# A decode attention kernel: one exponential per group of heads, the head masks as products, and output scaling on GpSimd

## The chip, the cores and the metric

The kernel runs on one core of one Trainium2 chip. The metric is device time in microseconds for one execution. The core's engines work side by side and wait for each other through semaphores: TensorE (PE in the profile, with its weight loads as PEld), VectorE (DVE), ScalarE (ACT), GpSimd (POOL) and SyncE (SP), which here issues nearly all transfers. Sixteen DMA engines move the data.

## The reference, cut to what matters

One token (B = S = 1) of width 512 passes through an attention block A over a window of W = 4096 cached keys and values, with 32 heads of width 128 and no sharing of heads, and through a small MLP block B whose result gates A's.

```python
xn = layernorm(x)
q = (xn @ wq).reshape(32, 128)
k, v = k_cache[:, Sk - 4096:, :], v_cache[:, Sk - 4096:, :]     # 32 heads each
scores = einsum("hd,hkd->hk", q, k) * 128 ** -0.5
o = einsum("hk,hkd->hd", softmax(scores), v)
s = o.reshape(4096) @ wo
out = x + s * silu(B(xn, w1, w2, w3, w4))
```

The window of K and of V is 33.5 MB each in bf16, the weights are about 12 MB, and each byte is used once.

## The kernel before, in words

**Groups.** The 32 heads are worked in 8 groups of G = 4. One K tile (`kv` in `k_pool`, three buffers) holds the 4096 keys of four heads: partition p belongs to head p mod 4 of the group and holds CP = 128 consecutive keys of 128 numbers, 4 MB in all. V has the same layout, with two buffers. The mask `par` (128 x 4) is 1 where the partition is of that head.

**Scores.** In `k_vector` DVE does 64 or 80 of the 128 keys of each partition, in four parts: a product K x q (L321) and a reduction over the 128 numbers (L323), into columns of the tile S. The rest goes through PE: `k_turn` transposes keys (L339), ACT copies them out of PSUM (L342), and `k_scores` multiplies them with q (L350) into `sT`, in which each partition holds its keys' scores with all four heads of the group, of which only its own head's is wanted.

**Softmax.** `sm_own` (L359, four ACT products) multiplies `sT` with the mask `par`, and `sm_max` adds the four up into S (L364, DVE) and takes each partition's maximum (L366). `sm_turn` transposes the maxima (L372, PE), takes the maximum of each head (L374) and writes it, scaled, into the first row of `md` (L376). `sm_exp` multiplies `md` with `par_t` on PE (L381): each partition gets four biases, one for each head, and for the three heads that aren't its own the bias is about −1e30, so that their exponentials are zero. ACT copies the biases (L384) and does four exponentials with sums (L388) into `pT`. `sm_den` adds the sums over the partitions (L394, PE) and `sm_rden` takes the reciprocals (L399, DVE).

**Values.** `v_wide` (L427) multiplies pT with V on PE, ACT copies the result (L433), `v_turn` transposes it (L444), `v_add` adds up the diagonal pieces into `oT` (L450, DVE), and `v_out` scales with `rden`: groups 0 to 2 by four ACT products (L475), groups 3 to 7 by one DVE product (L471). The last 32 columns of the last group use narrow matmuls instead (`v_part`, L461).

**Output.** `ox_spread` (L482, DVE), `ox_pick` (L490 PE; L492, L496 DVE) and `y_wide` (L518, PE) multiply blocks of 16, 8 and 4 heads with wo. The last four heads go through `y_head`. A product with the gate and a sum with x end the kernel.

**Order.** The order on PE, DVE and ACT is written out by hand (`tc.manual_schedule`); GpSimd's and SP's is not in that list. The loop over s = 0 to 9 does the scores of group s and the values of group h = s − 2. One step is, for DVE: K part 0, `sm_rden(s-2)`, K part 1, the two small instructions of `sm_turn(s-1)`, K part 2, `v_add(h-1)`, `v_out(h-1)`, in step 6 `ox_spread(0)`, K part 3, in step 6 the DVE part of `ox_pick(0)`, `sm_max(s)`. Step 7 takes `v_add` and `v_out` of groups 4 and 5, and `ox_spread(1)` follows the latter, before `sm_max(7)`. Step 8 begins with the pick of block 1 and `sm_turn(7)`, `sm_exp(7)`. SP issues the loads in program order (`load`, L76); a load into a buffer waits until its old contents have been read. One PSUM buffer (`misc`) serves the maxima, biases, denominators and transposed outputs in turn.

**Memory.** `pad` is an unused tile that moves what is allocated behind it.

Of the kernel before, what the change touches and what calls it, by code (L numbers as in the profile page):

```python
# [8 lines left out]
P = 128  # L9
BF16 = mybir.dt.bfloat16  # L10
FP32 = mybir.dt.float32
ACT = mybir.ActivationFunctionType
ALU = mybir.AluOpType
AX = mybir.AxisListType
# [4 lines left out]
G = 4  # L19
# [7 lines left out]
def kernel(  # L27
# [14 lines left out]
    nc = tc.nc  # L42
# [25 lines left out]
    ps_o = ctx.enter_context(tc.tile_pool(name="ps_o", bufs=1, space=PSUM))  # L68
    ps_y = ctx.enter_context(tc.tile_pool(name="ps_y", bufs=1, space=PSUM))
    sm_pool = ctx.enter_context(tc.tile_pool(name="sm", bufs=3))  # L70
    small.tile([P, 96], BF16, name="pad")
    wts_guard = tc.tile_pool(name="wts", bufs=1)
    wts = wts_guard.__enter__()

# [44 lines left out]
    ind = const.tile([P, 1], FP32, name="ind")  # L119
    nc.vector.tensor_reduce(out=ind[:], in_=ident_f[:, 0:P:32], axis=AX.X, op=ALU.max)  # L120
    neg_half = const.tile([P, 33], FP32, name="neg_half")
    nc.vector.memset(neg_half[:], -0.5)

# [102 lines left out]
                           in_=qt_ps[rows].bitcast(BF16).rearrange("p g (a m l) -> p g a m l", a=G, l=2)[:, :, :, 0, :])  # L226

    shifted_bf = small.tile([P, KC], BF16, name="shifted_bf")
    nc.vector.memset(shifted_bf[:], 0.0)
    hs_ps = ps_misc.tile([P, KC], FP32, tag="misc", name="hs_ps")  # L230
    for j in range(KC):
        for c in range(KC):
# [35 lines left out]
    for i, (col, w) in enumerate(terms):  # L268
# [26 lines left out]
    par = const.tile([P, G], FP32, name="par")  # L295
    nc.vector.tensor_reduce(out=par[:], in_=ident_f[:].rearrange("p (b a) -> p a b", a=G), axis=AX.X,
                            op=ALU.max)
    par_t = const.tile([1 + G, PB, G], FP32, name="par_t")
    nc.vector.tensor_scalar(out=par_t[:],
                            in0=ident_f[0:1 + G, 1:1 + G].unsqueeze(1).to_broadcast([1 + G, PB, G]),  # L300
                            scalar1=ident_f[0:1 + G, 0:1], scalar2=None, op0=ALU.add)
    md = const.tile([1 + G, G], FP32, name="md")
    nc.vector.tensor_scalar(out=md[:], in0=ident_f[0:1 + G, 1:1 + G], scalar1=-1.0, scalar2=1e30,
                            op0=ALU.add, op1=ALU.mult)

    st = {}

    def nd(g):
        return 64 if g == 0 or g >= LATE else 80

    def k_open(g):
        st[g] = {
            "sT": ps_s.tile([P, CP - 64, G], FP32, tag="sT", name="sT"),
            "S": sm_pool.tile([P, CP], FP32, tag="S", name="S"),
        }

    def k_vector(g, kn, part):
# [33 lines left out]
                                 lhsT=kt[:, i, l::2], rhs=q_pair[:, g, l, :], start=(l == 0), stop=(l == 1))  # L351


    def sm_own(g):
        s = st[g]
        m = CP - nd(g)
        s["own"] = sm_pool.tile([P, CP - 64, G], FP32, tag="own", bufs=1, name="own")
        for a in range(G):
            nc.scalar.mul(s["own"][:, 0:m, a], s["sT"][:, 0:m, a], par[:, a:a + 1])  # L359

    def sm_max(g):
        s = st[g]
        n = nd(g)
        nc.vector.tensor_reduce(out=s["S"][:, n:CP], in_=s["own"][:, 0:CP - n, :], axis=AX.X, op=ALU.add)  # L364
        s["m1"] = sm_pool.tile([P, 1], FP32, tag="m1", name="m1")
        nc.vector.tensor_reduce(out=s["m1"][:], in_=s["S"][:], axis=AX.X, op=ALU.max)  # L366

    def sm_turn(g):

        s = st[g]  # L370
        mt_ps = ps_misc.tile([1, P], FP32, tag="misc", name="mt_ps")
        nc.tensor.transpose(mt_ps[:], s["m1"][:], ident_f[:])  # L372
        mx = sm_pool.tile([1, G], FP32, tag="mx", name="mx")
        nc.vector.tensor_reduce(out=mx[:], in_=mt_ps[:].rearrange("r (b a) -> r a b", a=G), axis=AX.X,  # L374
                                op=ALU.max)
        nc.vector.tensor_scalar(out=md[0:1, :], in0=mx[:], scalar1=-scale, scalar2=None, op0=ALU.mult)  # L376

    def sm_exp(g):
        s = st[g]
        mb_ps = ps_misc.tile([P, G], FP32, tag="misc", name="mb_ps")  # L380
        nc.tensor.matmul(mb_ps[:], lhsT=par_t[:].rearrange("k b a -> k (b a)"), rhs=md[:], start=True,  # L381
                         stop=True)
        mb = sm_pool.tile([P, G], FP32, tag="mb", name="mb")
        nc.scalar.copy(out=mb[:], in_=mb_ps[:])  # L384
        s["pT"] = sm_pool.tile([P, CP, G], BF16, tag="pT", name="pT")
        s["sum"] = sm_pool.tile([P, G], FP32, tag="sum", name="sum")
        for a in range(G):
            nc.scalar.activation(out=s["pT"][:, :, a], in_=s["S"][:], func=ACT.Exp, scale=scale,  # L388
                                 bias=mb[:, a:a + 1], accum_out=s["sum"][:, a:a + 1])

    def sm_den(g):
        s = st[g]
        s["den"] = ps_misc.tile([P, G], FP32, tag="misc", name="den_ps")
        nc.tensor.matmul(s["den"][:], lhsT=ones_f[:], rhs=s["sum"][:], start=True, stop=True)  # L394

    def sm_rden(g):
        s = st[g]
        s["rden"] = sm_pool.tile([P, G], FP32, tag="rden", name="rden")
        nc.vector.reciprocal(out=s["rden"][:], in_=s["den"][:])  # L399


# [44 lines left out]
    def v_add(g):  # L446
        s = st[g]
        if g < NG - 1:
            s["oT"] = sm_pool.tile([P, G], FP32, tag="oT", name="oT")
        nc.vector.tensor_reduce(out=s["oT"][:], in_=s["ot"][:].rearrange("p (x m) -> p m x", m=32)[:, 0:G, :],  # L450
                                axis=AX.X, op=ALU.add)

# [11 lines left out]
    def v_out(g):  # L464
        h = G * g
        b = [i for i, (h0, _) in enumerate(blocks) if h >= h0][-1]
        if b not in o_blk:
            o_blk[b] = sm_pool.tile([P, blocks[b][1]], BF16, tag=f"o{b}", bufs=1, name="o")
        c = h - blocks[b][0]
        if g >= NG - 5:  # L470
            nc.vector.tensor_tensor(out=o_blk[b][:, c:c + G], in0=st[g]["oT"][:], in1=st[g]["rden"][:],  # L471
                                    op=ALU.mult)
            return
        for k in range(G):
            nc.scalar.mul(o_blk[b][:, c + k:c + k + 1], st[g]["oT"][:, k:k + 1], st[g]["rden"][:, k:k + 1])  # L475


    def ox_spread(i):
# [52 lines left out]
    for s in range(NG + LAG):  # L531
# [22 lines left out]
        if s < NG:  # L554
            nb = len(batches(s))

            def keys(b0, b1):
                for b in range(b0, b1):
                    k_turn(s, kn, b)
                    if b > 0:  # L560
                        k_scores(s, b - 1)

            k_open(s)
            k_vector(s, kn, 0)
            keys(0, 2)
            if s == 7:
                v_turn(h - 1)
                v_add(h - 1)
                v_out(h - 1)
            elif s > 1:  # L570
                sm_den(s - 2)
                sm_rden(s - 2)
            elif s == 1:
                sm_max(0)
            k_vector(s, kn, 1)
            keys(2, 4)
            if s == 7:
                sm_den(h)
                sm_rden(h)
                keys(4, nb - 2)  # L580
                sm_turn(s - 1)
                keys(nb - 2, nb)
            else:
                if s > 0:
                    sm_turn(s - 1)
                keys(4, nb)
            k_scores(s, nb - 1)
            sm_own(s)
            if s == 7:
                k_vector(s, kn, 2)  # L590
                v_wide(h, v)
                sm_exp(s - 1)
                v_turn(h)
                y_open()
                k_vector(s, kn, 3)
                v_add(h)
                v_out(h)
                ox_spread(1)
                sm_max(s)
                continue  # L600
            if s > 0:
                sm_exp(s - 1)
            if h > 0:
                v_turn(h - 1)
            k_vector(s, kn, 2)
            if h >= 0:
                v_wide(h, v)
            if h > 0:
                v_add(h - 1)
                v_out(h - 1)  # L610
            if s == 6:
                ox_spread(0)
            k_vector(s, kn, 3)
            if s == 6:
                ox_pick(0)
            if s > 0:
                sm_max(s)
        elif s == NG:
            ox_pick(1)
            sm_turn(NG - 1)  # L620
            sm_exp(NG - 1)
            y_wide(1, False)
            sm_den(NG - 2)
            sm_rden(NG - 2)
            y_wide(0, False)
            warm(3)
            v_wide(h, v)
            sm_den(NG - 1)
            sm_rden(NG - 1)
            v_turn(h)  # L630
            v_add(h)
            v_out(h)
            ox_spread(2)
        else:
            v_open(h)
            warm(3)
            v_wide(h, v, cuts[1], last=False)
# [47 lines left out]
```

## Time and profile before

| | before |
|---|---|
| time, median of 3 runs | 193.25 us (193.23 to 193.55) |
| span of the profiled execution | 191.2 us |
| PE / PEld busy | 116.4 us (61%) / 74.2 us (39%) |
| DVE busy | 150.9 us (79%), 175 instructions |
| ACT busy | 89.2 us (47%), 191 instructions |
| POOL busy | 2.3 us (1%), 11 instructions |
| DMA | 79.02 MB, mean 413 GB/s |

The page gives the profiled execution by its span, from the first instruction to the end of the last; it states no device time of that same execution beside it. The median of the three timed runs is 2.05 us above the span. Rows of groups read: line, engine, operation, output <- inputs, shapes, count | busy us, mean ns of one | idle time before them and what ended it. Rows in order of time read: start us, duration us, then the same, with idle time before it in brackets. In windows, the busy time of each engine in that stretch stands with its count of instructions.

### The profile page before, as it was taken

What the parts mean: (1) busy time and instruction counts of PE and PEld (TensorE: products, weight loads), DVE (VectorE), ACT (ScalarE), POOL (GpSimd) and SP (SyncE); (2) the same over time, 40 slices, a digit from 0 to 9 for tenths busy, and PEclk for the clock granted to TensorE, in tenths of its full rate; (3) what the DMA queues carried; (4) which work ended last, traced back from release to release, by engine and by line L of the source; (5) the groups of instructions that cost most, each with busy time, mean ns of one, the idle gap of its engine ahead of it and who ended that gap; (6) DMA issues with size and microseconds to landing.
All of it is one profiled execution on the core that took longest, in us unless ns stands there. A gap on an engine that the chain in (4) does not pass through costs nothing.

```text
span 191.2 us, 2839 instructions
## 1 busy us (share of the span) xinstructions
PE 116.4 (61%) x1159; PEld 74.2 (39%) x1159; DVE 150.9 (79%) x175; ACT 89.2 (47%) x191; POOL 2.3 (1%) x11
## 2 busy tenths in 40 slices
PE   1653754989825368256845772680888189739762
PEld 0430222767614334143334441540763077313322
DVE  1660159979999999999999999999999999980111
ACT  2001370888794076427464564542475148733120
POOL 2110000000000000000000000000000000000000
PEclk9999695555755557955695588557567858975998
DMA  6999999999999999999999999999999998999990
GB/s 211 447 430 404 431 418 439 439 439 437 432 434 439 432 429 432 432 439 432 422 432 432 418 422 418 452 439 435 439 432 434 435 432 372 471 425 405 420 371 32
DMA packets 4572, 79.02 MB, mean 413 GB/s; under 512 B 624, under 2 KB 1232, under 8 KB 1488
## 3 DMA queue, kind: packets, MB, share of 16 engines
q1 hardware_dynamic: 4264, 74.65, 91.6%
q10 hardware_dynamic: 296, 4.20, 5.1%
q8 instruction: 9, 0.15, 0.3%
q14 instruction: 3, 0.02, 0.0%
HBM read 78.84 MB, written 0.00 MB: 412 GB/s over the span
## 4 chain that ended last, share of the span: by engine, by line
DVE 46%; DMA 43%; PE 5%; ACT 3%; issue 1%; SPq 1%; ACTq 0%; DVEq 0%
DMA kv<-in_A_k_cache_dram 31%; DVE S L323 28%; DVE prod L321 15%; DMA kv<-in_A_v_cache_dram 10%; ACT kt L342 3%; DMA x_bf<-in_A_x_dram 2%; PE pt L339 2%; PE ov L427 1%; DVE m L366 1%; DVE S L364 1%; SPq L76 1%; PE sT L350 1%; DVE mx L374 1%; PE oT L461 1%; PE ot_ps L444 0%
## 5 line engine op out<-in xcount | busy, mean ns | idle before, releaser
L323 DVE TENSOR_REDUCE S<-prod 128x20 f32<-128x2560 bf16 (+1 forms) x32 | 86.0, 2686 | 1.1
L342 ACT COPY kt<-pt 128x1024 bf16<-128x1024 bf16 x52 | 51.2, 1013 | 40.4 <-PE pt L339 38.7
L339 PE MATMUL pt<-ident_f,kv 128*128 128x128 f32 x208 | 46.7, 376 | 10.8 <-DMA kv<-in_A_k_cache_dram 10.8
L321 DVE TENSOR_TENSOR prod<-kv,q_bc 128x2560 bf16<-128x2560 bf16 (+1 forms) x32 | 45.4, 1418 | 3.9 <-DMA kv<-in_A_k_cache_dram 3.7
L339 PEld LDWEIGHTS pt<-ident_f,kv 128*128 128x128 f32 x208 | 34.2, 196 | 14.4 <-DMA kv<-in_A_k_cache_dram 10.5
L350 PE MATMUL sT<-q_pair,kt 128*128 128x8 bf16 x416 | 19.4, 170 | 15.7 <-ACT kt L342 15.5
L350 PEld LDWEIGHTS <-kt 128*128 128x128 bf16 x416 | 16.4, 104 | 26.8 <-ACT kt L342 25.8
L427 PE MATMUL ov<-kv,pT 128*16 128x512 bf16 x248 | 22.0, 515 | 1.4 <-DMA kv<-in_A_v_cache_dram 1.4
L388 ACT ACTIVATE pT<-S,mb 128x128 bf16<-128x128 f32 x32 | 13.9, 573 | 0.3
L372 PE MATMUL mt_ps<-ident_f,m 128*1 128x128 f32 x8 | 2.9, 359 | 17.4 <-DVE rden L399 16.9
L433 ACT COPY ov_sb<-ov 128x512 f32<-128x512 f32 x8 | 4.7, 586 | 17.1 <-PE ov L427 17.1
L427 PEld LDWEIGHTS <-pT 128*16 128x16 bf16 x248 | 6.9, 109 | 13.2 <-issue 11.4
L359 ACT ACTIVATE own<-sT,par 128x48 f32<-128x48 f32 (+1 forms) x32 | 7.5, 356 | 3.7 <-PE sT L350 3.7
L444 PE MATMUL ot_ps<-ident_f,ov_sb 128*128 128x128 f32 x32 | 7.1, 359 | 2.9 <-ACT mb L384 1.9
L211 DVE CAST q_row<-qr_ps 128x512 bf16<-128x512 f32 x1 | 0.7, 692 | 9.9 <-PE qr_ps L208 9.9
L388 ACT ACTIVATION_READ_ACCUMULATOR pT<-S,mb 128x1 f32 x32 | 8.3, 258 | 0.0
L372 PEld LDWEIGHTS mt_ps<-ident_f,m 128*1 128x1 f32 x8 | 0.6, 80 | 17.9 <-DVE rden L399 17.2
L399 DVE RECIPROCAL rden<-den_ps 128x4 f32<-128x4 f32 x8 | 1.4, 175 | 7.0 <-PE den_ps L394 7.0
L381 PE MATMUL mb_ps<-md,par_t 5*128 5x4 f32 x16 | 3.9, 311 | 4.1 <-DVE md L376 4.1
L255 ACT ACTIVATE a_row<-a_ps 128x384 bf16<-128x384 f32 x1 | 0.5, 491 | 12.0 <-remote 12.0
L444 PEld LDWEIGHTS ot_ps<-ident_f,ov_sb 128*128 128x128 f32 x32 | 4.5, 178 | 3.9 <-ACT mb L384 2.3
L208 PE MATMUL qr_ps<-wq_sb,xq_bf 128*1 128x512 bf16 x32 | 3.1, 566 | 3.7 <-DMA wq_sb<-in_A_wq_dram 3.7
(122 smaller groups left out, 81.6 us busy)
## 6 DMA issues: line engine op xcount, KB each, us to landing
kv<-in_A_k_cache_dram SPq DMA_DIRECT2D x7, 4096.0 KB, 31.3
kv<-in_A_v_cache_dram SPq DMA_DIRECT2D x7, 4096.0 KB, 30.6
wq_sb<-in_A_wq_dram ACTq DMA_DIRECT2D x1, 4096.0 KB, 17.6
kv<-in_A_k_cache_dram SPq DMA_DIRECT2D x2, 2048.0 KB, 27.4
wo<-in_A_wo_dram SPq DMA_DIRECT2D x1, 2048.0 KB
kv<-in_A_v_cache_dram SPq DMA_DIRECT2D x1, 2048.0 KB
kv<-in_A_v_cache_dram SPq DMA_DIRECT2D x2, 1024.0 KB, 17.6
w_sb<-in_B_w_dram SPq DMA_DIRECT2D x1, 1376.0 KB, 9.1
```

The lines of the kernel that those rows point to most:

```text
L321: nc.vector.tensor_tensor(out=prod[:, 0:m, :], in0=kn[:, rows, :], in1=q_bc[:, g:g + 1, :].to_broadcast([P, m, Dh]), op=ALU.mult)
L323: nc.vector.tensor_reduce(out=st[g]["S"][:, rows], in_=prod[:, 0:m, :], axis=AX.X, op=ALU.add)
L339: nc.tensor.transpose(pt[:, i, :], kn[:, c:c + 2, :].rearrange("p c d -> p (c d)").bitcast(FP32), ident_f[:])
L342: nc.scalar.copy(out=kts[b][:, 0:n, :], in_=pt[:, 0:n, :].bitcast(BF16))
L350: nc.tensor.matmul(st[g]["sT"][:, c:c + 2, :].rearrange("p c a -> p (c a)"), lhsT=kt[:, i, l::2], rhs=q_pair[:, g, l, :], start=(l == 0), ...
L359: nc.scalar.mul(s["own"][:, 0:m, a], s["sT"][:, 0:m, a], par[:, a:a + 1])
L372: nc.tensor.transpose(mt_ps[:], s["m1"][:], ident_f[:])
L381: nc.tensor.matmul(mb_ps[:], lhsT=par_t[:].rearrange("k b a -> k (b a)"), rhs=md[:], start=True, stop=True)
L388: nc.scalar.activation(out=s["pT"][:, :, a], in_=s["S"][:], func=ACT.Exp, scale=scale, bias=mb[:, a:a + 1], accum_out=s["sum"][:, a:a + 1])
L427: nc.tensor.matmul(ov[r:r + 4 * G], lhsT=s["pT"][:, c:c + 4, :].rearrange("p i a -> p (i a)"), rhs=v[:, c:c + 4, :], start=(i < 4), stop=( ...
L433: nc.scalar.copy(out=s["ov_sb"][:], in_=ov[:])
L444: nc.tensor.transpose(ot_ps[:, step * j:step * j + P], s["ov_sb"][:, j, :], ident_f[:])
```

## The change

- `sm_exp`: the bias is one number for each partition, its own head's maximum. One exponential with one sum gives `e`, and four ACT products of `e` with the columns of `par` give `pT`.
- `sm_turn` writes the scaled maxima 32 times over ([1, 32, 4]) so that one matmul brings each partition its own; `par_t` and `md` go.
- `sm_den`: each partition has one sum; the sums are broadcast as weights and multiplied with `par`.
- `sm_own` goes. `sm_max` multiplies `sT` with `par` in one DVE product before it adds up.
- `v_out`: groups 0 to 5 are scaled by one GpSimd product, groups 6 and 7 by DVE.
- `S`, `rden` and `oT` get eight buffers each; two memsets at the start go from DVE to GpSimd; `pad` is longer.

```diff
-    small.tile([P, 96], BF16, name="pad")
+    small.tile([P, 208], BF16, name="pad")
...
-    nc.vector.memset(neg_half[:], -0.5)
+    nc.gpsimd.memset(neg_half[:], -0.5)
...
-    nc.vector.memset(shifted_bf[:], 0.0)
+    nc.gpsimd.memset(shifted_bf[:], 0.0)
...
-    par_t = const.tile([1 + G, PB, G], FP32, name="par_t")
-    nc.vector.tensor_scalar(out=par_t[:], ...)
-    md = const.tile([1 + G, G], FP32, name="md")
-    nc.vector.tensor_scalar(out=md[:], ...)
...
-            "S": sm_pool.tile([P, CP], FP32, tag="S", name="S"),
+            "S": sm_pool.tile([P, CP], FP32, tag="S", bufs=NG, name="S"),
...
-    def sm_own(g):
-        s = st[g]
-        m = CP - nd(g)
-        s["own"] = sm_pool.tile([P, CP - 64, G], FP32, tag="own", bufs=1, name="own")
-        for a in range(G):
-            nc.scalar.mul(s["own"][:, 0:m, a], s["sT"][:, 0:m, a], par[:, a:a + 1])
-
     def sm_max(g):
         s = st[g]
         n = nd(g)
-        nc.vector.tensor_reduce(out=s["S"][:, n:CP], in_=s["own"][:, 0:CP - n, :], axis=AX.X, op=ALU.add)
+        own = sm_pool.tile([P, CP - 64, G], FP32, tag="own", bufs=1, name="own")[:, 0:CP - n, :]
+        nc.vector.tensor_tensor(out=own, in0=s["sT"][:, 0:CP - n, :],
+                                in1=par[:].unsqueeze(1).to_broadcast([P, CP - n, G]), op=ALU.mult)
+        nc.vector.tensor_reduce(out=s["S"][:, n:CP], in_=own, axis=AX.X, op=ALU.add)
...
-        nc.vector.tensor_scalar(out=md[0:1, :], in0=mx[:], scalar1=-scale, scalar2=None, op0=ALU.mult)
+        s["mx"] = sm_pool.tile([1, PB, G], FP32, tag="mxr", bufs=1, name="mxr")
+        nc.vector.tensor_scalar(out=s["mx"][:], in0=mx[:].unsqueeze(1).to_broadcast([1, PB, G]), scalar1=-scale,
+                                scalar2=None, op0=ALU.mult)
...
-        mb_ps = ps_misc.tile([P, G], FP32, tag="misc", name="mb_ps")
-        nc.tensor.matmul(mb_ps[:], lhsT=par_t[:].rearrange("k b a -> k (b a)"), rhs=md[:], start=True,
-                         stop=True)
-        mb = sm_pool.tile([P, G], FP32, tag="mb", name="mb")
+        mb_ps = ps_misc.tile([P, 1], FP32, tag="misc", name="mb_ps")
+        nc.tensor.matmul(mb_ps[:], lhsT=s["mx"][:].rearrange("k b a -> k (b a)"), rhs=one_f,
+                         start=True, stop=True)
+        mb = sm_pool.tile([P, 1], FP32, tag="mb", name="mb")
         nc.scalar.copy(out=mb[:], in_=mb_ps[:])
+        e = sm_pool.tile([P, CP], BF16, tag="e", bufs=1, name="e")
         s["pT"] = sm_pool.tile([P, CP, G], BF16, tag="pT", name="pT")
-        s["sum"] = sm_pool.tile([P, G], FP32, tag="sum", name="sum")
+        s["sum"] = sm_pool.tile([P, 1], FP32, tag="sum", name="sum")
+        nc.scalar.activation(out=e[:], in_=s["S"][:], func=ACT.Exp, scale=scale, bias=mb[:], accum_out=s["sum"][:])
         for a in range(G):
-            nc.scalar.activation(out=s["pT"][:, :, a], in_=s["S"][:], func=ACT.Exp, scale=scale,
-                                 bias=mb[:, a:a + 1], accum_out=s["sum"][:, a:a + 1])
+            nc.scalar.mul(s["pT"][:, :, a], e[:], par[:, a:a + 1])
...
-        nc.tensor.matmul(s["den"][:], lhsT=ones_f[:], rhs=s["sum"][:], start=True, stop=True)
+        nc.tensor.matmul(s["den"][:], lhsT=s["sum"][:].to_broadcast([P, P]), rhs=par[:],
+                         start=True, stop=True)
...
-        s["rden"] = sm_pool.tile([P, G], FP32, tag="rden", name="rden")
+        s["rden"] = sm_pool.tile([P, G], FP32, tag="rden", bufs=NG, name="rden")
...
-            s["oT"] = sm_pool.tile([P, G], FP32, tag="oT", name="oT")
+            s["oT"] = sm_pool.tile([P, G], FP32, tag="oT", bufs=NG, name="oT")
...
-        if g >= NG - 5:
+        if g >= NG - 2:
             nc.vector.tensor_tensor(out=o_blk[b][:, c:c + G], in0=st[g]["oT"][:], in1=st[g]["rden"][:],
                                     op=ALU.mult)
             return
-        for k in range(G):
-            nc.scalar.mul(o_blk[b][:, c + k:c + k + 1], st[g]["oT"][:, k:k + 1], st[g]["rden"][:, k:k + 1])
+        nc.gpsimd.tensor_tensor(out=o_blk[b][:, c:c + G], in0=st[g]["oT"][:], in1=st[g]["rden"][:], op=ALU.mult)
...
             k_scores(s, nb - 1)
-            sm_own(s)
```

More of the change, by code (lines that the diff above doesn't have):

```diff
@@ L297 @@
                             op=ALU.max)
-    par_t = const.tile([1 + G, PB, G], FP32, name="par_t")
-    nc.vector.tensor_scalar(out=par_t[:],
-                            in0=ident_f[0:1 + G, 1:1 + G].unsqueeze(1).to_broadcast([1 + G, PB, G]),
-                            scalar1=ident_f[0:1 + G, 0:1], scalar2=None, op0=ALU.add)
-    md = const.tile([1 + G, G], FP32, name="md")
-    nc.vector.tensor_scalar(out=md[:], in0=ident_f[0:1 + G, 1:1 + G], scalar1=-1.0, scalar2=1e30,
-                            op0=ALU.add, op1=ALU.mult)
     st = {}
```

## The prediction

> **What bounds the kernel now.** I read the busy shares by slice first, then the busy times of chosen windows, then the order in time on VectorE (DVE) and on TensorE (PE) near the end. The slices show two engines full at once:
>
> ```profile
> DVE  1660159979999999999999999999999999980111
> DMA  6999999999999999999999999999999998999990
> ```
>
> Windows give the degree (the columns are PE, weight loads, DVE, ACT and POOL busy, then the granted PE clock, the DMA share and GB/s):
>
> ```profile
> 60.00:78.00 18.00, 10.16 (x110) 6.52 (x109) 17.76 (x14) 9.39 (x21) 0.00 (x0) 0.62 1.01 434
> 97.00:115.00 18.00, 11.22 (x119) 7.22 (x116) 17.83 (x14) 9.92 (x24) 0.00 (x0) 0.72 1.00 429
> 170.00:186.30 16.30, 12.05 (x116) 4.91 (x116) 2.90 (x14) 3.67 (x12) 0.00 (x0) 0.81 0.94 397
> ```
>
> The 16 DMA engines are saturated until 186.3 us. DVE is busy 17.8 of 18 us in the middle, and only after 171.6 us is it mostly idle. ACT is half idle. The end is set by the last V transfer, as the chain of waits in order of time says:
>
> ```profile
> 167.79 18.54 DMA kv<-in_A_v_cache_dram
> 186.33 0.05 issue
> 186.38 0.97 PE oT L461 x32
> ```
>
> So two questions matter. Do the transfers stay saturated? And how late may DVE be before PE is late for the last V pieces? For the first, I added up the bytes issued and the packets moved in the trace: whenever a K or V load is issued after 30 us, at least 3.7 MB are still outstanding. The least is 3.73 MB at 166.55 us, before the first piece of the last V load, which is 8.6 us of work at 435 GB/s. A K load may thus be released several microseconds later at no cost.
>
> For the second, DVE's order shows where it waits for data (the bracket is idle time and its cause):
>
> ```profile
> 133.34 0.29 DVE L366 TENSOR_REDUCE m<-S 128x1 f32<-128x128 f32 x1
> 134.17 1.49 DVE L321 TENSOR_TENSOR prod<-kv,q_bc 128x2560 bf16<-128x2560 bf16 x1 [0.55 <-DMA kv<-in_A_k_cache_dram]
> ...
> 153.49 0.34 DVE L364 TENSOR_REDUCE S<-own 128x48 f32<-128x192 f32 x1
> 153.87 0.29 DVE L366 TENSOR_REDUCE m<-S 128x1 f32<-128x128 f32 x1
> 154.07 1.22 DVE L321 TENSOR_TENSOR prod<-kv,q_bc 128x2048 bf16<-128x2048 bf16 x1
> ```
>
> From 41.9 us, when the second K tile landed, DVE runs back to back; its one wait for data is 0.55 us, for group 6. Group 7's keys land at 153.5 us, before DVE is ready. Everything added to DVE therefore piles up until its last softmax step, with 0.55 us of relief. PE's waits at the end are the only other relief:
>
> ```profile
> 179.67 0.81 PE L507 MATMUL wm<-zero_bf 128*128 128x512 bf16 x3
> 181.50 1.04 PE L427 MATMUL ov<-kv,pT 128*16 128x512 bf16 x16 [1.02 <-DMA kv<-in_A_v_cache_dram]
> 183.93 0.61 PE L427 MATMUL ov<-kv,pT 128*16 128x512 bf16 x8 [0.41 <-DMA kv<-in_A_v_cache_dram]
> 186.38 0.96 PE L461 MATMUL oT<-pT,kv 128*128 128x4 bf16 x32 [0.17 <-DMA kv<-in_A_v_cache_dram]
> ```
>
> PE's queue is in order. In step 8 it is held by the transpose of group 7's maxima (L372, 170.77 us), which needs DVE, and then does L381, the wide output products, L394, the warm matmuls, group 6's V products and so on to 181.5 us with only short waits that themselves follow that chain. A DVE that is late by d makes the end late by d − (1.02 + 0.41 + 0.17) = d − 1.60 us.
>
> **The change part by part.** The prices come from these groups (busy us, mean ns):
>
> ```profile
> L492 DVE TENSOR_TENSOR pick<-ox_ps,mh 128x256 f32<-128x256 f32 x1 | 0.4, 414 | 0.0
> L492 DVE TENSOR_TENSOR pick<-ox_ps,mh 128x64 f32<-128x64 f32 x1 | 0.2, 215 | 0.0
> L376 DVE TENSOR_SCALAR md<-mx 1x4 f32<-1x4 f32 x8 | 1.2, 156 | 0.3
> L299 DVE TENSOR_SCALAR par_t<-ident_f 5x128 f32<-5x128 f32 x1 | 0.3, 266 | 0.0
> L471 DVE TENSOR_TENSOR o<-oT,rden 128x4 bf16<-128x4 f32 x5 | 0.8, 163 | 1.4 <-PE oT L461 1.2
> L178 POOL TENSOR_TENSOR ln_rstd_x<-ln_rstd_x,neg_half 128x1 f32<-128x1 f32 x1 | 0.6, 554 | 5.7 <-DVE ln_rstd_x L176 5.7
> masks.py:199 POOL TENSOR_SCALAR_AFFINE_SELECT ident_f<-ident_f 128x128 f32<-128x128 f32 x1 | 0.3, 293 | 0.0
> ```
>
> *Head masks.* The four ACT products of `sm_own` become one DVE product in `sm_max`, PSUM times a broadcast mask: the same kind as L492. Its two shapes give (414 − 215)/192 = 1.04 ns an element, so 0.348 us for 192 elements and 0.414 for 256. The reduction L364 must wait for it (0.04 us, the gap between 153.49 + 0.34 and 153.87). Groups 1 to 6 pay 0.39, groups 0 and 7 0.45: 6 x 0.39 + 2 x 0.45 = 3.24 us. The lower end leaves the gaps out, 2.92; the upper is the sum itself. Queued behind it are L364, the maximum L366 and the next group's K product, all of DVE's stream.
>
> *Maxima.* L376 writes 128 values in place of 4. L299 did that in 266 ns against 156: +0.11 each, 8 x 0.11 = 0.88 us (ends 0 and 1.04, the latter at 1.04 ns an element).
>
> *Output scaling.* Groups 0 to 2 move from ACT to POOL and touch no one before step 6. Group 4's product leaves DVE: its follower started 0.11 us after oT's end and could start 0.08 before it, −0.19. Groups 3 and 5 are followed at once by `ox_spread` on DVE, which now waits for POOL; the rest of step 6 and, in step 7, the last maximum stand behind that wait. Handing DVE to POOL took 0.08 us (7.42 to 7.50) and back 0.04 (8.05 to 8.09). POOL's product lies between 0.10 (its smallest memset) and 0.55 us (L178, which is a power); I take 0.29, the simple operation over 128 elements, which is nearer in kind. That is 0.41 us from oT to the spread, against 0.30 (147.65 to 147.95) and 0.24 (169.47 to 169.71): +0.11 and +0.17. With group 4, +0.10 in all (ends −0.28 and +0.62).
>
> [...]
>
> *Exponentials.* Four exponentials with four accumulator reads (0.57 and 0.26 us, one pair each 0.39) become one pair and four products. The `own` products, four in 0.92 us for 48 elements and 1.00 for 64, give about 0.28 us pitch at 128. So all of pT is ready some 1.9 us after `mb` instead of 1.74. ACT as a whole loses about 1 us a group with `sm_own`. I cost this at nothing: pT of group g is used a step later, and group 7's was complete at 174.3 us and used at 181.5. Without that cover it would cost 0.2 us once. On PE, L381 with one column and L394 with a broadcast weight keep their two passes; nothing either way.
>
> *Setup.* Four small DVE instructions go (0.09 + 0.06 + 0.27 + 0.15 us), two of them to POOL. They precede the wait for keys at 26.1 us, which swallows them.
>
> Sum: d = 3.24 + 0.88 + 0.10 − 0.55 = 3.67 us at DVE's end. Minus 1.60, the end moves 2.07 us. K loads go out up to 3 us later and the last V load 3.3 us later, against 8.6 us outstanding: no hole. The profiled span was 191.2 us and the median of the runs 193.25, so 2.05 us lie outside the span and stay. 191.2 + 2.07 + 2.05 = 195.3 us.
>
> With all low ends d = 2.92 + 0 − 0.28 − 0.55 = 2.09, +0.5 us: 193.7. With all high ends d = 3.24 + 1.04 + 0.62 − 0.55 = 4.35, +2.75: 196.0. PE's clock adds to it: the same three warm matmuls took 1.07 us at 175.6 and 0.81 at 179.7, and work moved by 3 us meets other clocks; I allow 0.6 us on the high side.
>
> **The rivals.** *Hidden after all, 193.3 us.* If DVE's lateness at the end is below 1.60 us, the last V piece still decides and nothing is seen. For it: the transfers are full to 186.3 us, and the waits of 0.55 and 1.60 us exist. Against it: the product alone must then cost under 0.27 us a group, where its row says 0.39. *POOL stops DVE, about 198 us.* If each of the four products of groups 0, 1, 2 and 4 blocked DVE's concurrent product for 0.55 us, d would grow by 2.2, and by 0.52 more at POOL's high price: 3.67 + 2.72 − 1.60 = +4.8. [...] *Faster, about 192.5 us.* V buffers move to other addresses and the last 16 us run at 397 GB/s where 435 is usual; at 418, the rate of several slices, they would end 0.8 us sooner. It decides only if DVE is not late, so it needs the first rival too. The byte counts and pieces are unchanged, and nothing else speaks for it.
>
> **How the numbers follow.** 0.2% is 0.39 us, about what a measurement of this kernel can tell from no change. DVE late and seen, 193.7 to 196.6: 0.75. Hidden: 0.13. POOL stops DVE: 0.06. Faster: 0.06. The range takes the hidden case in and leaves the last two mostly out: 193.1 to 196.6. Faster 0.06, same 0.13, slower 0.81.
>
> **What would show it.** In the changed profile: a DVE product of 0.35 us before each L364-like reduction; K's first product of group 7 near 157 us rather than 154.07; the last maximum near 174.5 rather than 170.3; PE's waits for V pieces in the last 7 us gone, with the final oT matmuls starting after the last landing by some 2 us; DMA still full to about 186 us. It is wrong if those waits are still there, or if DMA shows a hole before 180 us.

## The result, and the profile after

The changed kernel takes 196.55 us (median of 6 runs, 195.61 to 197.46) against 193.43 us for the kernel before (6 runs, 193.23 to 193.94): ratio 1.016 [1.0139, 1.0181]. It is slower by 3.1 us. The forecast was 195.3 us with a range of 193.1 to 196.6, so the direction and the path held; the size came out 1.25 us short, 0.05 us under the upper end of the range, and 0.18 of the 1.25 is that the kernel before stood at 193.25 in the forecast. The six runs lie in two groups, three from 195.61 to 195.96 and three from 197.14 to 197.46. The profiled execution, with 197.21 us and a span of 195.3 us, is of the upper group, 4.1 us of span above the profile of before, so what is read from it is more than what the median lost.

The slices of the page answer the first question of the prediction: DMA is still full, without a hole, to the slice that ends at 185.5 us, while DVE is busy to about 176 us where it had ended at about 171.

```profile
DVE  1650169979999999999999999999999998961021
DMA  6998999999999999999999999999999999999910
```

The last V packet ended at 185.85 us (before: 185.93). The transfers have not moved; what comes after them has. The chain of waits in order of time (start, duration, step) no longer holds a V transfer. It goes through PE's queue of step 8:

```profile
174.90 0.29 DVE m L355
...
175.38 0.39 PE mt_ps L361
...
180.29 1.39 PE wm L499 x3
181.69 2.68 PE ov L420 x28
...
190.54 0.96 PE oT L454 x32
```

So the transposed maxima of group 7 started at 175.38 us instead of 170.77, and the last narrow V products (`v_part`) at 190.54 instead of 186.38, 4.16 us later. That is the whole difference of the spans.

DVE in order of time (start, duration; the bracket is idle time and its cause), at the end of group 6 and the end of group 7:

```profile
155.74 0.35 DVE L351 TENSOR_TENSOR own<-sT,par 128x192 f32<-128x192 f32 x1
156.13 0.35 DVE L353 TENSOR_REDUCE S<-own 128x48 f32<-128x192 f32 x1
156.51 0.29 DVE L355 TENSOR_REDUCE m<-S 128x1 f32<-128x128 f32 x1
156.72 1.22 DVE L314 TENSOR_TENSOR prod<-kv,q_bc 128x2048 bf16<-128x2048 bf16 x1
...
173.32 0.23 DVE L443 TENSOR_REDUCE oT<-ot_ps 128x4 f32<-128x64 f32 x1 [1.36 <-PE ot_ps L437]
173.86 0.23 DVE L474 TENSOR_TENSOR spread<-o,mt 128x64 bf16<-128x64 bf16 x1 [0.31 <-POOL o L467]
174.00 0.42 DVE L351 TENSOR_TENSOR own<-sT,par 128x256 f32<-128x256 f32 x1
174.45 0.42 DVE L353 TENSOR_REDUCE S<-own 128x64 f32<-128x256 f32 x1
174.90 0.29 DVE L355 TENSOR_REDUCE m<-S 128x1 f32<-128x128 f32 x1
```

The new product is the first line of each half, 0.35 and 0.42 us, with its reduction right behind it. Group 7's first key product stands at 156.72 us (before 154.07) and the last maximum at 174.90 (before 170.29). The wait in the line at 173.32 is new: DVE, the engine that everything waited for, itself waits 1.36 us for PE. In the kernel before, the same instruction had no bracket:

```profile
169.26 0.21 DVE L450 TENSOR_REDUCE oT<-ot_ps 128x4 f32<-128x64 f32 x1
...
170.29 0.29 DVE L366 TENSOR_REDUCE m<-S 128x1 f32<-128x128 f32 x1
```

Why PE was late there is in its own order of time, step 7:

```profile
160.44 0.39 PE L386 MATMUL den_ps<-par,sum 128*128 128x4 f32 x2 [1.04 <-DVE oT L443]
...
163.98 0.37 PE L361 MATMUL mt_ps<-ident_f,m 128*1 128x128 f32 x1 [1.15 <-DVE rden L392]
...
167.82 3.59 PE L420 MATMUL ov<-kv,pT 128*16 128x512 bf16 x32
...
172.17 1.11 PE L437 MATMUL ot_ps<-ident_f,ov_sb 128*128 128x128 f32 x4 [0.25 <-ACT mb L375]
```

PE now waits twice for the late DVE, about 1 us each time. In the kernel before, neither `den_ps` nor `mt_ps` waited there, and the 32 V products of group 5 took 1.90 us:

```profile
159.28 0.36 PE L394 MATMUL den_ps<-sum,ones_f 128*128 128x4 f32 x2
...
161.54 0.27 PE L372 MATMUL mt_ps<-ident_f,m 128*1 128x128 f32 x1
...
164.60 1.90 PE L427 MATMUL ov<-kv,pT 128*16 128x512 bf16 x32
...
170.77 0.37 PE L372 MATMUL mt_ps<-ident_f,m 128*1 128x128 f32 x1 [0.54 <-DVE pick L492]
```

After the change the same 32 take 3.59, while the granted clock is at half. In the traces of the two kernels, what lies between one change of the clock and the next is 3.41 us or a whole multiple of it (up to 20.48 us before, up to 23.89 after), and the windows below are cut at these times (the columns are as in the prediction: the length of the stretch, PE busy first, and after POOL the granted PE clock, 1.00 for full and 0.50 for half). First the kernel before, then the one after:

```profile
159.06:162.47 3.41, 3.10 (x49) 2.42 (x48) 2.98 (x6) 3.08 (x4) 0.00 (x0) 1.00 0.83 356
162.47:165.89 3.42, 2.53 (x49) 1.50 (x49) 3.35 (x3) 2.79 (x6) 0.00 (x0) 1.00 1.09 456
165.89:169.30 3.41, 1.80 (x19) 0.88 (x11) 3.38 (x3) 2.38 (x10) 0.00 (x0) 0.99 1.01 436
169.30:172.71 3.41, 1.53 (x12) 0.78 (x12) 2.01 (x10) 0.30 (x2) 0.00 (x0) 0.50 1.04 452
```

```profile
155.97:159.39 3.42, 3.42 (x34) 2.92 (x31) 3.32 (x5) 1.92 (x3) 0.00 (x0) 0.50 1.00 431
159.39:162.80 3.41, 1.89 (x27) 1.57 (x26) 3.38 (x4) 2.12 (x3) 1.11 (x1) 1.00 0.90 384
162.80:166.21 3.41, 2.26 (x19) 1.91 (x17) 2.88 (x6) 1.45 (x2) 0.00 (x0) 0.50 1.16 489
166.21:169.63 3.42, 2.63 (x37) 1.27 (x40) 3.38 (x2) 1.11 (x2) 0.00 (x0) 0.50 0.98 423
169.63:173.04 3.41, 3.16 (x26) 1.63 (x16) 2.29 (x2) 1.51 (x6) 0.00 (x0) 0.50 1.02 442
```

In these rows, at full clock, a stretch with 3.10 or 2.53 us of PE work keeps the clock, and one with 1.80 or 1.89 us loses it for the next stretch. At half clock, the stretch with 3.42 us (155.97) gets it back, and those with 2.26 to 3.16 us do not. The busy time alone does not decide, though: at full clock the kernel before kept the clock with 1.98 us (from 182.92), and the changed kernel lost it with 2.48 (from 115.04); at half clock the changed kernel did not get it back with 3.41 us (from 176.45). What else counts is not shown here. In the changed kernel the first wait for DVE empties the stretch from 159.39 to 1.89 us, the clock is lost at 162.80 and comes back only at 183.3, six stretches later. Before, it had been lost for two stretches only, from 169.30 to 176.1.

### The profile page after: what moved, and what is told of

Read it like the earlier page. It is cut to its first block, busy times and chain, and to the rows that moved or that the text cites. A ratio compares the mean times of both kernels' runs of the same rounds, so it can differ in the third digit from the quotient of the medians.

```text
span 195.3 us, 2791 instructions
## 1 busy us (share of the span) xinstructions
PE 121.1 (62%) x1159; PEld 75.5 (39%) x1159; DVE 153.7 (79%) x176; ACT 81.8 (42%) x131; POOL 8.2 (4%) x19
## 4 chain that ended last, share of the span: by engine, by line
DVE 62%; DMA 21%; issue 7%; PE 7%; POOL 1%; ACT 1%; SPq 0%; ACTq 0%; POOLq 0%; DVEq 0%
DVE S L316 36%; DMA kv<-in_A_k_cache_dram 19%; DVE prod L314 18%; DMA x_bf<-in_A_x_dram 2%; PE ov L420 2%; PE yr_ps L510 2%; DVE S L353 2%; DVE own L351 1%; PE wm L499 1%; DVE m L355 1%; DVE mxr L366 1%; DVE mx L363 1%; PE ot_ps L437 1%; POOL o L467 1%; PE oT L454 0%
## 5 line engine op out<-in xcount | busy, mean ns | idle before, releaser
L332 PE MATMUL pt<-ident_f,kv 128*128 128x128 f32 x208 | 46.0, 371 | 5.2 <-DMA kv<-in_A_k_cache_dram 5.2
L332 PEld LDWEIGHTS pt<-ident_f,kv 128*128 128x128 f32 x208 | 33.7, 193 | 8.8 <-DMA kv<-in_A_k_cache_dram 4.9
L420 PE MATMUL ov<-kv,pT 128*16 128x512 bf16 x248 | 25.2, 577 | 0.0
L467 POOL TENSOR_TENSOR o<-oT,rden 128x4 bf16<-128x4 f32 x6 | 5.6, 940 | 154.9 <-DVE oT L443 154.9
L381 ACT ACTIVATE pT<-e,par 128x128 bf16<-128x128 bf16 x32 | 11.9, 568 | 0.3
L437 PE MATMUL ot_ps<-ident_f,ov_sb 128*128 128x128 f32 x32 | 8.0, 395 | 2.4 <-ACT mb L375 1.2
L372 PE MATMUL mb_ps<-ones_f,mxr 1*128 1x1 f32 x16 | 4.2, 332 | 6.1 <-DVE mxr L366 6.1
L375 ACT COPY mb<-mb_ps 128x1 f32<-128x1 f32 x8 | 1.3, 159 | 14.2 <-PE mb_ps L372 14.2
L372 PEld LDWEIGHTS mb_ps<-ones_f,mxr 1*128 1x128 f32 x16 | 3.8, 292 | 7.6 <-PE sT L343 5.8
L437 PEld LDWEIGHTS ot_ps<-ident_f,ov_sb 128*128 128x128 f32 x32 | 5.1, 197 | 3.4 <-ACT ov_sb L426 1.7
```

What stands on the lines that cost most here:

```text
L332: nc.tensor.transpose(pt[:, i, :], kn[:, c:c + 2, :].rearrange("p c d -> p (c d)").bitcast(FP32), ident_f[:])
L372: nc.tensor.matmul(mb_ps[:], lhsT=s["mx"][:].rearrange("k b a -> k (b a)"), rhs=one_f, start=True, stop=True)
L381: nc.scalar.mul(s["pT"][:, :, a], e[:], par[:, a:a + 1])
L420: nc.tensor.matmul(ov[r:r + 4 * G], lhsT=s["pT"][:, c:c + 4, :].rearrange("p i a -> p (i a)"), rhs=v[:, c:c + 4, :], start=(i < 4), stop=( ...
L437: nc.tensor.transpose(ot_ps[:, step * j:step * j + P], s["ov_sb"][:, j, :], ident_f[:])
L467: nc.gpsimd.tensor_tensor(out=o_blk[b][:, c:c + G], in0=st[g]["oT"][:], in1=st[g]["rden"][:], op=ALU.mult)
```

## The experiments

The kernel before took 193.33 to 193.46 us beside them. Where dummy matmuls are added, their results go unused.

### The head masks back on ACT, all else as changed

```diff
+            nc.scalar.mul(s["own"][:, 0:m, a], s["sT"][:, 0:m, a], par[:, a:a + 1])   # in sm_own, four times
...
-        nc.vector.tensor_tensor(out=own, in0=s["sT"][...], in1=par[...], op=ALU.mult)   # in sm_max
```

> The changed kernel with the head masks back on ACT (sm_own and the four products per group as before; the VectorE product taken out); all else of the change stays. Theory A, VectorE is late: the eight products (0.35 to 0.42 us plus 0.04 each, 3.2 us in all) are most of the lateness, which was 2.65 us at group 7's first product (156.72 against 154.07). Without them that product starts at 154 to 154.4 and PE again waits for V's pieces: 193.2 to 193.8 us. Rival B, the new exponentials or the GpSimd scaling set the time: it stays above 195.5 us.

193.13 us (192.79 to 193.64), ratio 0.9978 [0.9967, 0.9989], just under the expected range. PE's order at the end has its waits for V back:

```profile
181.32 1.04 PE L424 MATMUL ov<-kv,pT 128*16 128x512 bf16 x16 [0.39 <-DMA kv<-in_A_v_cache_dram]
...
186.19 0.96 PE L458 MATMUL oT<-pT,kv 128*128 128x4 bf16 x32 [0.16 <-DMA kv<-in_A_v_cache_dram]
```

Group 7's first key product is at 154.06 us, as before the change. So the loss goes with the product. Everything else in the change, taken together, costs nothing that is seen: the last maximum is 0.85 us late here (171.14 us against 170.29), and PE's waits for V take that up, the first of them down from 1.02 to 0.39 us. This version is 0.2% faster than the kernel before, and it is the best one found. Why it is a little faster isn't shown; its last V packet ended 0.1 us sooner.

### The output scaling back on ACT and DVE, all else as changed

```diff
-        if g >= NG - 2:
+        if g >= NG - 5:
...
-        nc.gpsimd.tensor_tensor(out=o_blk[b][:, c:c + G], in0=st[g]["oT"][:], in1=st[g]["rden"][:], op=ALU.mult)
+        for k in range(G):
+            nc.scalar.mul(o_blk[b][:, c + k:c + k + 1], st[g]["oT"][:, k:k + 1], st[g]["rden"][:, k:k + 1])
```

> The changed kernel with the output scaling as before (groups 0 to 2 on ACT, 3 to 7 on VectorE). Theory A: VectorE gains 0.25 us at group 3's scaling and 0.2 at group 5's and loses 0.15 at group 4's; the time stays within 0.5 us of the changed kernel, 195.6 to 197.0 us. Rival B, GpSimd's products (up to 1.38 us each beside VectorE) hold VectorE or the blocks of outputs up: it falls to 194 us or less.

196.26 us (195.47 to 197.36), ratio 1.0148 [1.0118, 1.0178]; the changed kernel's 1.016 lies within that interval. GpSimd's part makes no difference that these runs can tell. The profiled execution (195.92 us, span 194.0) is like the lower group of the changed kernel's runs. Its DVE is just as late at group 7's first product (156.78 us), but the clock was at half from 160.69 to 170.93 us only, three stretches instead of six, and DVE waited less for PE:

```profile
172.82 0.23 DVE L443 TENSOR_REDUCE oT<-ot_ps 128x4 f32<-128x64 f32 x1 [0.61 <-PE ot_ps L437]
```

### The VectorE product alone, in the kernel before

```diff
-            sm_own(s)
...
+        nc.vector.tensor_tensor(out=own, in0=s["sT"][:, 0:CP - n, :],
+                                in1=par[:].unsqueeze(1).to_broadcast([P, CP - n, G]), op=ALU.mult)
```

> The kernel before with one part of the change alone: the four ACT products of sm_own replaced by the one VectorE product in sm_max. Theory A: VectorE is late by 6 products less the wait of 0.55 us at group 7's first product (about 2.2 us) and by 2.7 us at its end; PE's waits for V take 1.6 off, a slow PE clock near the end adds 0 to 1.2: 194.3 to 195.6 us. Rival C, the lateness is hidden and something else of the change costs the time: 193.2 to 193.6 us.

196.65 us (195.79 to 197.69), ratio 1.015 [1.0125, 1.0176]: the whole loss from this one edit, and above what was expected. Group 7's first product stands at 156.73 us, as in the changed kernel, and step 7 has the same late V products (3.59 us) at the same half clock. The expectation counted too little for the clock, as the prediction did, and too little lateness: it had put group 7's first product about 2.2 us late, and 2.66 were measured, of which 0.21 lies in a later landing of group 1's keys (first product at 42.12 us instead of 41.91).

### The product twice

```diff
         nc.vector.tensor_tensor(out=own, in0=s["sT"][...], in1=par[...], op=ALU.mult)
+        nc.vector.tensor_tensor(out=own, in0=s["sT"][...], in1=par[...], op=ALU.mult)
```

> The changed kernel with the VectorE product of the head masks done twice in each group (the same result). Theory A: another 6 x 0.35 + 0.45 = 2.6 us of lateness at group 7's first product (near 159.4 us) and 3.0 at the end, none of it hidden any more: 199.0 to 200.3 us. The last V load then goes out near 174 us with under 1 us of other transfers left, so a small hole may add to it. Rival: part of the loss is a fixed wait that the product's presence brings, not its length: under 198 us.

200.48 us (199.43 to 201.09), ratio 1.0362 [1.0338, 1.0386], just above the expected range. DVE in order of time:

```profile
159.33 1.22 DVE L314 TENSOR_TENSOR prod<-kv,q_bc 128x2048 bf16<-128x2048 bf16 x1
```

That is 2.61 us after the changed kernel's 156.72, and seven products (six at 0.39, one at 0.45) make 2.79: a second product delays DVE by about as much as the first, and no slack is left. The last V packet, at 188.88 us, is 3.0 us late here, but PE reached V's last piece later still.

### PE kept busy in step 7

```diff
+                warm_tr(2)                 # two dummy matmuls of 512 columns
                 sm_den(h)
                 sm_rden(h)
                 keys(4, nb - 2)
+                warm_tr(3)                 # three more
                 sm_turn(s - 1)
```

> The changed kernel with five matmuls of zeros of 512 columns in step 7, where PE waits for VectorE (two before the denominators of group 5, three before the transpose of group 6's maxima). Theory G, the granted clock: PE's 2.2 us of waiting there drop the clock to 0.5 from 162.8 to 183.3 us, which makes group 5's V products 3.6 us long instead of 1.9, VectorE wait 1.4 us for them, and the products of step 8 another 1.2 us late. With PE kept busy the clock stays at 1.0 to 169 us or later, and the time falls by 1 to 2 us against the changed kernel: 194.4 to 195.7 us. Rival: the clock only follows, the lateness of VectorE alone decides: 196.2 to 197.0 us.

194.95 us (194.22 to 196.19), ratio 1.009 [1.0062, 1.0119]: 1.6 us below the changed kernel's median, with nothing taken off DVE; against the kernel before beside each, the loss is 1.62 us instead of 3.12. The windows, cut at this run's own clock times, show why (they lie 0.1 us from those of the changed kernel's profile, so the two can be compared):

```profile
159.50:162.90 3.40, 2.43 (x29) 1.62 (x28) 3.37 (x4) 2.13 (x3) 1.11 (x1) 1.00 0.91 388
162.90:166.30 3.40, 2.33 (x28) 1.50 (x26) 2.97 (x6) 1.96 (x3) 0.00 (x0) 1.00 1.18 499
166.30:169.70 3.40, 2.50 (x42) 1.27 (x43) 3.33 (x3) 1.07 (x4) 0.00 (x0) 1.00 0.98 424
169.70:173.10 3.40, 1.07 (x6) 0.58 (x6) 3.05 (x5) 1.93 (x6) 0.20 (x1) 1.00 0.99 419
```

With 2.33 us and more in the first three stretches the clock stays at 1.00 until 173.1, where the fourth, with 1.07 us, loses it. Group 5's V products then take 1.90 us at 167.04, DVE does not wait for `ot_ps`, and the last maximum is at 173.34 instead of 174.90. So about half of the loss, 1.5 of 3.1 us, was the clock.

### Fewer keys on DVE

```diff
-        return 64 if g == 0 or g >= LATE else 80
+        return 64 if g == 0 or g >= LATE else 76
```

> The changed kernel with 76 in place of 80 keys per partition on VectorE in groups 1 to 6 (the other 52 through PE). Each key costs VectorE (1.48 + 2.82)/20 = 0.215 us, so 0.86 us less per group, more than the 0.5 us a group that the change added. Theory A: VectorE waits for K's arrival again, the last V piece decides: 193.1 to 193.8 us. Rival D, PE or ACT, with more transposes and copies, become late instead: 194.5 us or more.

194.66 us (194.38 to 195.24), ratio 1.0059 [1.0041, 1.0076], in the rival's range but not for its reason. DVE was on time (group 7's first product at 153.77 us), and PE, which was to become late, waited for V at the end as it never had:

```profile
185.12 0.61 PE L420 MATMUL ov<-kv,pT 128*16 128x512 bf16 x8 [1.70 <-DMA kv<-in_A_v_cache_dram]
```

The last four V packets ended one by one, 0.31 us apart and up to 1.2 us after all others (187.09 us), as if one DMA engine were late. The shift of keys to PE adds matmuls, and one queue of the page, q8 instruction, brings nine packets of 16 KB each (0.15 MB in all) in the kernel before, where PE has 2318 instructions, half of them weight loads. That these packets are PE's instructions is the author's inference; with 256 more of them, below, ten packets come. The ninth piece came at 182.9 us instead of 187.1, before V's end rather than behind it. Two theories of that followed: that the place of the ninth piece near the end costs the 1.2 us, or that having nine pieces before V's end does.

### Dummy matmuls in the kernel before, and a whole piece more

All three add one-column matmuls in steps 2 to 5: 36 to the kernel before, 92 to the kernel with 76 keys, 128 to the kernel before (128 matmuls with their weight loads are 256 instructions, for which the last of the three runs shows one piece of 16 KB more).

```diff
+                if 2 <= s <= 5:
+                    idle_pe(9)             # 23 and 32 in the other two
                 if s > 0:
                     sm_turn(s - 1)
```

> The kernel before with 36 one-column matmuls of zeros, nine in each of steps 2 to 5, where PE waits for VectorE; nothing else is changed and their results are not used. In the run with 76 keys VectorE was on time, yet the time was 1.2 us up: a 16 KB instruction fetch began at 182.9 us (187.1 in the kernel before), and one DMA engine's last V packets ended 1.2 us after the rest, at 187.1 us. Theory F: PE's 72 more instructions moved that fetch into the last V pieces, so these dummies do the same: 194.2 to 195.0 us. Rival D: PE or ACT work of the extra keys cost it: 193.2 to 193.7 us here.

194.76 us (194.54 to 195.35), ratio 1.0074 [1.0059, 1.0088]. DVE has nothing more to do in this kernel. The ninth piece came at 184.7 us, the last V packets, again 0.3 us apart, ended at 187.11, and `v_part` waited 0.91 us for them.

> The changed kernel with 76 keys on VectorE in groups 1 to 6, and 92 one-column matmuls of zeros (23 in each of steps 2 to 5): 72 + 184 = 256 more PE instructions than before, one whole fetch of 16 KB, so the last fetch falls where the kernel before had it. Theory F: 193.1 to 193.7 us. Rival D (the extra keys cost the time): 194.5 us or more.

194.56 us (194.33 to 195.02), ratio 1.0062 [1.0049, 1.0076]. The last piece now comes at 187.5 us, behind V's end as before the change, and the last V packets are late all the same (187.06 us). The theory of the place falls. The time is in rival D's range, but extra keys can't be needed for the loss: the kernel with 36 dummies has none of them and lost as much.

> The kernel before with 128 one-column matmuls of zeros (32 in each of steps 2 to 5), 256 more PE instructions: one whole 16 KB fetch more, the last one again after V's last packets (near 187 us), as in the kernel before. Theory F (place): only a fetch in the last microseconds of V costs: 193.2 to 193.7 us. Theory F2 (number), formed on the run with 76 keys and 92 dummies: nine instead of eight fetches before V's end put two of them on one DMA engine, wherever they fall: 194.3 to 195.0 us, with one engine's last V packets about 1.2 us behind the others.

194.69 us (194.49 to 195.12), ratio 1.0062 [1.0046, 1.0078], as theory F2 expected. The page's queue of instructions has ten pieces here and nine in the kernel before; the last again comes at 188.1 us, behind V's end:

```profile
q8 instruction: 10, 0.16, 0.3%
```

PE's order at the end waits for one V piece after another:

```profile
177.98 1.90 PE L427 MATMUL ov<-kv,pT 128*16 128x512 bf16 x32 [0.93 <-DMA kv<-in_A_v_cache_dram]
...
187.54 0.96 PE L461 MATMUL oT<-pT,kv 128*128 128x4 bf16 x32 [0.16 <-DMA kv<-in_A_v_cache_dram]
```

So nine pieces before V's end instead of eight cost 1.2 to 1.4 us in these three kernels (1.43, 1.23 and 1.27 against the kernel before beside each), wherever the ninth fell. A piece takes about 1 us (0.96 to 1.10 us each in the kernel before; all nine are 0.3% of 16 engines' 191.2 us), and PE's last wait for V ends 0.44 or 0.45 us after the latest packet (187.10 and 187.54 us in the last of these; 185.93 and 186.38 in the kernel before). That the ninth goes to an engine that already had one of the others would explain it; the trace names neither the engine of a piece nor that of a V packet, so this is inferred. It is a cost of the repair by 76 keys, and no part of the loss measured above, which needs no late packet.

### Fewer keys in two groups only

```diff
-        return 64 if g == 0 or g >= LATE else 80
+        return 64 if g == 0 or g >= LATE else 76 if g in (5, 6) else 80
```

> The changed kernel with 76 instead of 80 keys on VectorE in groups 5 and 6 only: 2 x 0.86 us less on VectorE and 24 more PE instructions, few enough that the ninth fetch stays behind V's last packets. Theory A: VectorE is about 0.9 us late at group 7's first product (near 155.0 us) instead of 2.65, which PE's waits for V hide: 193.2 to 194.0 us. Rival: the product's presence, or the keys moved to PE, cost the time whatever VectorE's lateness: 194.5 us or more.

194.60 us (193.44 to 195.65, 12 runs), ratio 1.0057 [1.0036, 1.0078]: only the lowest runs are in the expected range, and the median is in the rival's. The last V packet is on time (185.75 us) and group 7's first product only 1.03 us late, but in the profiled execution (195.56 us) the clock stayed at half from 154.4 to 181.7 us:

```profile
154.40:181.70 27.30, 23.16 (x190) 12.97 (x192) 17.77 (x25) 12.58 (x23) 1.31 (x2) 0.50 0.99 423
```

> The changed kernel with 76 keys on VectorE in groups 5 and 6 and the five matmuls of zeros in step 7, the two edits together. With 76 keys in two groups alone the median was 194.6 us in runs from 193.4 to 195.7, and its profile had VectorE only 1.0 us late at group 7's first product, but a clock of 0.5 from 154.4 to 181.7 us. Theories A and G together: lateness under 1.6 us is hidden once the clock stays up, so 193.2 to 193.8 us and a spread under 1 us. Rival: 194.4 us or more, the product costs time even when VectorE is in time and PE at full clock.

With the five dummy matmuls of step 7 as well: 194.10 us (193.58 to 194.32, 11 runs), ratio 1.0029 [1.0018, 1.004]. The runs spread over 0.7 us instead of 2.2, and both sets of V products take 1.90 us. Against the kernel before beside each, the dummies take the loss from 1.18 to 0.75 us. The time lies between the two expected ranges, so it settles neither by itself. The last maximum is 2.66 us late (172.95), a part of it through the dummies themselves: group 7's third key product starts at 164.35 us against 162.24 before, behind a wait of 1.42 us for `mt_ps`.

## Why the prediction came out as it did

**The path.** Right. The prediction said that the end moves by DVE's lateness at the last softmax, less 1.60 us of PE's waits for V, and that PE's clock adds to it. The profiles with different edits agree with that sum, which takes the measured lateness as given; how that came about follows below. Lateness is the start of group 7's `mt_ps` less 170.77 us; clock is what the three warm matmuls and the 32 V products of group 6 took beyond 1.07 and 1.90 us; the end is the start of `v_part` less 186.38.

| kernel | lateness | − 1.60 + clock | sum | end moved |
|---|---|---|---|---|
| changed | 4.61 | −1.60 + 0.39 + 0.82 | 4.22 | 4.16 |
| scaling back on ACT and DVE | 4.03 | −1.60 + 0.39 + 0.04 | 2.86 | 2.81 |
| product alone | 4.75 | −1.60 + 0.39 + 0.83 | 4.37 | 4.63 |
| changed, PE kept busy | 3.05 | −1.60 + 0.37 | 1.82 | 1.75 |
| 76 keys in two groups | 3.00 | −1.60 + 0.39 + 0.80 | 2.59 | 2.53 |
| the same, PE kept busy | 2.65 | −1.60 + 0.18 | 1.23 | 1.17 |
| product twice | 7.01 | −1.60 + 0.26 | 5.67 | 5.61 |

All but one lie within 0.07 us. With the product alone, `v_part` waits another 0.43 us for DVE's `oT`, which the sum leaves out.

**The product.** Priced right: 347 to 349 ns for 192 elements and 418 for 256, against 0.348 and 0.414; and 0.39 us with the gap (156.13 − 155.74). The edit alone carried the loss.

**The maxima.** Priced too high. Group of the tile, durations in ns (minimum, median, maximum):

```profile
L366 DVE TENSOR_SCALAR mxr<-mx x8: 214/214/215, 51.9 to 176.1; 1x128 f32<-1x128 f32 x8
```

With the key product starting 0.14 us after it instead of 0.08, the cost was 0.06 us each, 0.48 in all instead of 0.88.

**The output scaling.** Priced too high by 0.20 us on DVE, with GpSimd's product itself priced too high. POOL in order of time:

```profile
131.29 1.38 POOL L467 TENSOR_TENSOR o<-oT,rden 128x4 bf16<-128x4 f32 x1 [17.31 <-DVE oT L443]
149.97 0.20 POOL L467 TENSOR_TENSOR o<-oT,rden 128x4 bf16<-128x4 f32 x1 [17.30 <-DVE oT L443]
```

With DVE waiting for it, it took 0.20 us, not 0.29. From the end of oT to the spread, 0.32 us now lie against 0.30 and 0.24 before: +0.02 and +0.08, and group 4's product saved 0.20 (its follower starts 2.45 us late where the product ahead of it was 2.65 late). That makes −0.10 instead of +0.10. Where a key product was running, POOL took 1.38 us (three times) or 1.11 us (once) and ended 0.06 or 0.05 us after it, while the key product kept its 1.48 or 1.22 us:

```profile
131.13 1.48 DVE L314 TENSOR_TENSOR prod<-kv,q_bc 128x2560 bf16<-128x2560 bf16 x1
```

That product of DVE started 0.16 us before POOL's and took as long as the one at 128.70 us in the kernel before, 1.48 us; POOL's was the one that took longer.

**The exponentials.** Hidden, as costed: group 7's pT was complete at 179.2 us and first used at 186.3.

**The wait of 0.55 us.** Gone, as costed: group 6's first key product, at 136.35 us, has no bracket.

**PE's clock and what follows from it.** This is the term that failed. By the terms just measured, DVE's own lateness is 3.24 + 0.48 − 0.10 − 0.55 = 3.07 us, and with PE kept busy it was 3.05, against the 3.67 that were predicted. Less 1.60, that would have put the end at +1.45 us, below the +2.07 of the sum. What brings it to +3.1 in the median is the clock, of which the prediction allowed 0.6 us and only on the high side. It was worth about 1.5 us in the median by the kernel that keeps PE busy. In the profiled execution it cost 1.56 us through the maxima (174.90 against 173.34) and 1.21 us through the warm matmuls and V products of step 8, less the 0.37 that stays with PE kept busy. The prediction looked at the work at the end, which would merely meet another clock. It did not ask who waits for DVE *in step 7*: PE's `den_ps` and `mt_ps` stand in its queue behind DVE's `oT` and `rden` and waited 1.04 and 1.15 us for them, and with these waits the clock was lost for what came behind them. The two errors, 0.62 us too much on DVE and about 1.5 us too little on PE, partly cancelled; that the time is still inside the range is luck. It is luck too that the sign "the last maximum near 174.5" came out: by the prediction's own sum it would be 170.29 + 3.67 = 173.96 us, the wait of 0.55 us having been left off, and the measured 174.90 is 173.34 with the clock's 1.56.

**The queue of transfers.** The last V load went out at 171.45 us instead of 166.55, 4.9 us later and not 3.3, since `v_wide` of group 5 frees its buffer and was slowed as well. With 3.6 us of work still outstanding there was no hole, as said. With the product twice V ended 3.0 us late, so the reserve ends about there.

**The rivals.** "Hidden" needed a product under 0.27 us a group; it took 0.39. No run shows the term of "POOL stops DVE", a hold of 0.55 us on DVE: beside GpSimd's products the key products kept their 1.48 and 1.22 us. "Faster" is what the change without its product does, by 0.2%, but not shown to be by the way that was named: its last V packet ended 0.1 us sooner, not 0.8.

## What to carry to other kernels

When an engine that is full is made later, list who waits for it in every stage, not only at the end: here two waits, of 1.04 and 1.15 us, cost TensorE half its clock for 20.5 us in the profile, and in the median that cost about as much as the lateness itself. Price moved work by the engine that receives it; ScalarE, with a share of 47%, gave up 7.4 us in the change as a whole, while the mask product put 3.2 us on the one engine without slack. Where the last load of a saturated stream set the end, as in the kernel before, even added TensorE instructions had a price, 1.43 us for 72 and 1.27 us for 256 of them, so a repair that moves work there should be read for late packets.

## What the runs showed of the hardware

- From one change of TensorE's granted clock to the next there lay 3.41 us or a whole multiple of it, up to 20.48 us in the profile before and 23.89 us after. In the changed kernel's stretch from 159.39 us, with waits of 1.04 and 0.48 us, 1.89 us of work lost the clock, and 2.43 us in the same stretch, with dummy matmuls, kept it. No threshold in busy time holds throughout: 1.98 us kept it elsewhere (before, from 182.92 us) and 2.48 lost it (after, from 115.04 us); at half clock 3.41 us once did not get it back (after, from 176.45 us).
- The changed kernel's runs lie in two groups, 195.6 to 196.0 and 197.1 to 197.5 us. That the place of the stretches against the kernel's start decides between them is a guess that no run tested. Two profiles fit it. With the scaling back, the stretches lay 1.3 us from those of the changed kernel's profile (160.69 against 159.39), the clock was at half for 10.2 us instead of 20.5, and the span was 1.3 us shorter. With the product alone they lay within 0.1 us, and the span of 195.8 us is like that of the upper group.
- With one more 16 KB piece on the queue of instructions before V's end, four kernels took 194.56 to 194.76 us, 1.2 to 1.4 us above the kernel before, though a piece takes only about 1 us (0.96 to 1.10 us each in the kernel before).
- A GpSimd product of 128 x 4 elements took 0.20 us with no DVE product beside it (149.97 and 173.62 us) and 1.11 to 1.38 us beside a DVE product of two SBUF operands, which was not slowed (1.48 us before and after for 2560 elements, 1.22 us for 2048).
